# Eight attention steps left undivided, their sums turned by TensorE and multiplied into the values

## The chip, the cores and the metric

The kernel runs on one core of a Trainium2 chip. A core has five engines that each work through a queue of their own in order: TensorE (PE in the profile, its weight loads PEld), VectorE (DVE), ScalarE (ACT), GpSimd (POOL) and SyncE (SP), which here issues nearly all the DMAs. [...] The metric is the time of one execution on the device in microseconds (us), as the median of several runs.

## The reference

```python
scale = 1.0 / np.sqrt(q.shape[-1])
scores = scale * np.matmul(q, k.transpose(0, 1, 3, 2))
thresh = np.max(scores, axis=-1, keepdims=True) - tau
scores = np.where(scores >= thresh, scores, -1000000000.0)
scores = scores - np.max(scores, axis=-1, keepdims=True)
attn = np.exp(scores)
attn = attn / (np.sum(attn, axis=-1, keepdims=True) + 1e-09)
return np.matmul(attn, v).astype(np.float32)
...
x = np.ascontiguousarray(attn_out.transpose(0, 2, 1, 3)).reshape(B * S, H * D)
h = x @ w_in
g = np.where(h > 0.0, h, alpha * (np.exp(np.minimum(h, 0.0)) - 1.0))
return (g @ w_out).astype(np.float32)
```

There are 8 sequences of 8 heads, 576 tokens and a head dimension of 64. Scores that lie more than tau under the maximum of their row are dropped; the rest goes through a softmax. The result, 4608 tokens by 512, goes through a network with 2048 hidden units and an ELU. All is fp32. The division by the sum is the line that the change touches: a row of weights is divided by its own sum, and then multiplied by the values.

## The kernel before, in words

Two heads of a sequence form a pair (`pr`, 32 in all). A step `(pr, i)` is a block of 128 queries of both heads; `i` is 0 to 3 for the four whole blocks and 4 (`NC`) for the 64 queries of each head that are left, which share one block. A step does this: TensorE makes the scores (`scores`, L673), VectorE the maximum of each row (`max_of`, L730). Then a row is masked in one of two forms, chosen for each step and head by the set `MASK_ACT`:

- VectorE's form: the threshold on GpSimd (`bound_of`, L734), the exponential on ScalarE (`exp_of`, L768), and on VectorE a compare-and-multiply that also sums the row (`mask_of`, L775).
- ScalarE's form: the threshold on VectorE (`pivot_of`, L746 or L748), a steep Prelu on ScalarE that sinks what lies under the threshold (`sink_of`, L753), and on ScalarE again an exponential that also sums the row (`raise_of`, L759). Here the Prelu needs the threshold, so it waits for VectorE twice: for the maximum, and for the threshold made from it.

The two sums are added up with a tiny constant (`total_of`, L783, or `total_act`, L720) and turned over (`reciprocal_of`, L789). Each head's 128x576 weights are multiplied by 1/sum on GpSimd (L726), ScalarE (`ACT_NORM`, L714) or VectorE (`NORM_DVE`, L709). TensorE turns the weights by 128x128 transposes (`turn_parts`, L792) in three parts, and each part is copied out of PSUM (a task called `put`, L808), by ScalarE or, for the parts in the set `PUT_DVE`, by VectorE. When all the steps of half a pair have their turned weights, TensorE multiplies them by the values (`values`, L925 and L930), and ScalarE copies the result to the tile `xt` (`values_out`, L1060), from which the network's first product reads.

In the first sequence the steps are ordered by their number n: n = 0 to 7 are blocks 0 and 1 of the pairs 0 to 3, n = 8, 9, 10 are blocks 2, 3 and 4 of pair 0, and so on. The first product of the network on the first 256 tokens (`ffn1`, L1102) can start once the values of n = 0 to 7 are there. Beside the steps, the 64-bit weights of the network are loaded and made fp32 in 32 pieces (tasks `lw`, `rest`, `shift`, `add`, `sign`, `end`; L485 to L518).

What is done when is fixed before the run. `early_tasks` gives every task a due time, from a formula plus entries of the table `MOVED`, sorts by it, and issues the tasks in that order; a task first issues all those that it needs, so a task with a late due time comes in just before the first task that needs it. The order in which tasks are issued is the order in which each engine's queue holds their instructions. In the stretch that matters below, the order by due time is: the maxima of step 6 (both heads), `end` of weight piece 0, the third part of step 4 with the copy out of pair 1's values, then `mask` of (6, 0) at 53, `mask` of (6, 1) at 54, and the three `put`s of step 5 at 55. The threshold of (6, 1) has the due time 914, so it is issued when `mask` of (6, 1) asks for it.

PSUM sets two more orders. Transposed parts and values share a pool of two buffers (tag `rt`): `room_for` issues whatever empties the older buffer before it gives out a new one.

```python
def room_for(pool, release):
    while len(taken[pool]) >= 2:
        taken[pool].popleft()()
    taken[pool].append(release)
```

So the third part of a step waits for the copy of the first part, and the values for an earlier part's copy. The scores have three buffers, one for each head: the scores of a step wait until the mask (VectorE's form) or the Prelu (ScalarE's form) has read the buffer's last content. `IDLES` puts some spare transposes of a constant into TensorE's queue.

Of the kernel before, what the change touches and what calls it, by code (L numbers as in the profile page):

```python
# [10 lines left out]
FP32 = mybir.dt.float32  # L11
# [4 lines left out]
ALU = mybir.AluOpType  # L16
# [7 lines left out]
 (7, 2)}  # L24
SU_ACT = {3, 13, 15, 20, 23, 25, 26, 29, 30, 31, 32, 33, 34, 35, 37, 39, 44}
QK_PE = set()
MASK_ACT = {(0, 0), (0, 1), (1, 1), (2, 0), (7, 1), (8, 0), (9, 1), (12, 1), (13, 0), (14, 1), (15, 0), (15, 1), (17, 0),
# [11 lines left out]
SCALE_ACT = {3, 6, 7, 9}  # L39
SUM_POOL = {0, 3}  # L40
SPLIT = {(4, 10)}
PUT_DVE = {(0, 2), (6, 2), (12, 0), (12, 1), (14, 1), (14, 2), (16, 1), (17, 2), (20, 1), (21, 0), (26, 0), (29, 0), (33,
 1), (33, 2), (34, 1)}

HEADS_APART = {(0, 0), (0, 1)}
# [323 lines left out]
def kernel(  # L369
# [22 lines left out]
    KJ = DM // P  # L392
    NFT = DF // P
    NPAIR = H // 2
# [8 lines left out]
    xpool = ctx.enter_context(tc.tile_pool(name="xpool", bufs=2))  # L403
# [312 lines left out]
    def total_act(pr, i, hs):  # L716
# [2 lines left out]
        st["summed"] = True  # L719
        nc.scalar.activation(st["su"][:, cs], st["sm"][:, cs, 0], AF.Identity, bias=st["sm"][:, 0, 1:2])  # L720

    def normalize(pr, i, hs):
        st = open_steps[pr, i]
        for h in hs:
            wv = st["w"][:, h * S : (h + 1) * S]
            nc.gpsimd.tensor_scalar(wv, wv, st["rs"][:, h : h + 1], 1.0, ALU.mult, ALU.mult)  # L726
# [64 lines left out]
    def transpose(dst, src):  # L791
        nc.tensor.matmul(dst, src, idents[-1], is_transpose=True, skip_group_check=True)  # L792
# [104 lines left out]
    def fetch(pr, i):  # L897
# [11 lines left out]
        else:  # L909
# [2 lines left out]
                back.rearrange("k (a b) n -> k a b n", b=2),  # L912
            )

    def values(pr, part, pv=None):
        b, j = divmod(pr, NPAIR)
        vm, vd = (raws[pr][x] for x in ("vm", "vd"))
        wT = wTs.pop((pr, part))
        if b not in xts:
            xts[b] = xpool.tile([P, KJ, MAIN], FP32, name="xt")  # L920
        n = wT.shape[1] * T
        if pv is None:
            pv = psum["t"].tile([P, 512], FP32, name="pv", tag="rt")
        watch = on_banks if wide else lambda *a: None
        watch(nc.tensor.matmul(pv[:, :n], vd, wT[:, :, NC], start=True, stop=False, skip_group_check=True), pv[:, :n])  # L925
        for c in range(NC):
            for h in range(2):
                g0, g1 = (2 * h, 2 * h + 10) if part else (0, 2 * NT)
                o = pv[h * D : (h + 1) * D, g0 * T : g1 * T]
                watch(nc.tensor.matmul(o, vm[:, h, c], wT[:, g0:g1, h * (NC + 1) + c], start=False, stop=(c == NC - 1),  # L930
                                       skip_group_check=True), o)
        return lambda: values_out(pr, part, pv)

    wide, turned_by = [], []
# [120 lines left out]
    def values_out(pr, part, pv):  # L1055
        b, j = divmod(pr, NPAIR)
        q0, n = TAIL * part, (3 if part else 2) * NT * T
        watch = on_banks if wide else lambda *a: None
        o = pv[:, q0 : q0 + 2 * P]
        watch(nc.scalar.copy(xts[b][:, j, part * 2 * P : (part + 1) * 2 * P], o), o)  # L1060
# [114 lines left out]
    steps = [(pr, i) for pr in range(NP) for i in ((0, 1, NC, 2, 3) if pr >= JOINED else range(NB))]  # L1175
    steps[:per_seq] = [(pr, i) for x in ((0, 1), (2, 3, NC)) for pr in range(NPAIR) for i in x]
    LATE = 10

    def behind(pr, i):
        if i in (1, NB - 1):  # L1180
# [126 lines left out]

    def early_tasks():
# [161 lines left out]
        for n in range(MIDDLE):  # L1470
# [16 lines left out]
            for h in hs:  # L1487
                task(("max", n, h), at_(0.2 + 0.5 * h, 1.8 + 0.6 * h, 0.8 + 0.5 * h), f"max{h}{k}", lambda pr=pr, i=i, h=h: max_of(pr, i, h), ("sc", n))
                back = ("turned", n - (2 if last_ else WBUFS)) if n >= WBUFS else None
                t_exp, t_th, t_mask = (at_(0.3 + 0.7 * h, 2.0 + 0.6 * h, 1.0 + 0.5 * h), at_(0.4 + 0.7 * h, 2.2 + 0.6 * h, 1.1 + 0.5 * h),  # L1490
                                       at_(2.0 + 1.6 * h, 5.6 + 0.1 * h, 4.0 + 0.1 * h))
                if (n, h) in MASK_ACT:
                    task(("exp", n, h), t_exp, f"exp{h}{k}", lambda pr=pr, i=i, h=h: sink_of(pr, i, h), ("th", n, h), back, "late" if last_ else None)
                    task(("th", n, h), t_th, f"th{h}{k}", lambda pr=pr, i=i, h=h: pivot_of(pr, i, h), ("max", n, h))
                    task(("mask", n, h), t_mask, f"mask{h}{k}", lambda pr=pr, i=i, h=h: raise_of(pr, i, h), ("exp", n, h))
                else:
                    task(("exp", n, h), t_exp, f"exp{h}{k}", lambda pr=pr, i=i, h=h: exp_of(pr, i, h),
                         ("max", n, h), exps[-1] if exps else None, ("mask", *exps[-2][1:]) if len(exps) > 1 else None)
                    task(("th", n, h), t_th, f"th{h}{k}", lambda pr=pr, i=i, h=h: bound_of(pr, i, h), ("max", n, h))
                    exps.append(("exp", n, h))  # L1500
                    task(("mask", n, h), t_mask, f"mask{h}{k}", lambda pr=pr, i=i, h=h: mask_of(pr, i, h), ("exp", n, h), ("th", n, h),
                         ("mask", n, 0) if h and (n, 0) not in MASK_ACT else back, "late" if last_ else None)
                scaled = normalize_act if (n, h) in ACT_NORM else normalize_dve if (n, h) in NORM_DVE else normalize_pool
                norm = lambda pr=pr, i=i, h=h, f=scaled: f(pr, i, h)
                task(("norm", n, h), at_(5.0 + 0.8 * h, 6.2 + 0.1 * h, 5.4 + 0.1 * h), f"norm{h}{k}", norm, ("rec", n))
            task(("su", n), at_(3.8, 5.8, 4.4), f"su{k}", lambda pr=pr, i=i, hs=hs, f=total_act if n in SU_ACT else total_of: f(pr, i, hs), *[("mask", n, h) for h in hs])
            task(("rec", n), at_(3.8, 5.8, 4.4), f"rec{k}", lambda pr=pr, i=i, hs=hs: reciprocal_of(pr, i, hs), ("su", n))
# [37 lines left out]
            if i in (1, NC) and n < MIDDLE - 4:  # L1545
                got = []
                mine_ = [number[pr, x] for x in ((0, 1) if i == 1 else (2, 3, NC))]

                def run_values(pr=pr, part=part, got=got):
                    room_for("t", lambda: do(("out", pr, part)))  # L1550
                    got.append(values(pr, part))

                def run_out(pr=pr, part=part, got=got):
                    got[0]()
                    if (pr, part) == (NPAIR - 1, 0):
                        push_ffn(0)
                    elif (pr, part) == (NPAIR - 1, 1):
                        push_ffn(1)

                m = n + 2  # L1560
                t_val, t_out = (begin[m] + 4.0, begin[m] + 6.2) if m < LATE else (begin[m] + 0.4, begin[m] + 3.3)
                if n < per_seq:
                    t_val, t_out = begin[n + 1] + 4.2, begin[n + 2] + 1.5
                    if n >= LATE:
                        t_val, t_out = begin[n + 1] + 5.6, begin[n + 1] + 6.8
                elif any(m in SQUARES for m in mine_):
                    t_val, t_out = begin[n + 3] + 5.7, begin[n + 3] + 5.8
                elif SWITCH + 1 >= m >= SWITCH:
                    t_val, t_out = t_val - 8.0, t_out - 8.0
                task(("val", pr, part), t_val, f"val{k}", run_values, *[("landed", m) for m in mine_], ("v", pr))  # L1570
                task(("out", pr, part), t_out, f"out{k}", run_out, ("val", pr, part), ("out", pr, 0) if part else None)
            if n == 0:
                task("idle", t + 2.1, None, lambda: idle(16))
            if n >= SWITCH:
# [777 lines left out]
```

## Time and profile before

| what | value |
|---|---|
| median of 3 runs | 1259.22 us (1258.13 to 1260.99) |
| the profiled execution's own time | 1259.32 us |
| span from its first to its last instruction | 1257.5 us |
| PE, DVE, ACT, POOL busy, share of the span | 99%, 83%, 51%, 58% |
| first matmul of the network (L1102) | 51.48 us |

The profile is of one execution. It gives busy times of each engine, the groups of instructions with their mean duration, the instructions in order of time with the idle time ahead of them and what ended it, and the chain of waits: the work that ended last, followed back link by link. Times in its rows count from the start of the span. "f" is a PSUM bank of the network, "sc" scores, "e" exponentials, "w" weights of the attention, "wTa" and "wTb" turned weights, "pv" values, "rt" turned parts, "mx" maxima, "th" thresholds, "rs" 1/sum.

### The profile page before, as it was taken

To read this page: it belongs to the slowest core of one execution; us is meant where nothing else is said; L and a number is where in the kernel's file an instruction comes from. 1 tells how busy PE (TensorE), PEld (TensorE's weight loads), DVE (VectorE), ACT (ScalarE), POOL (GpSimd) and SP (SyncE) were. 2 spreads that over 40 slices of the span, in tenths; PEclk is the share of its full clock that TensorE was granted. 3 is DMA by queue.
4 is the path that set the end of the run, shared out by engine and by line. 5 is a ranking of instruction groups with operands and counts; after the bars stand their busy time and mean duration, and the time that the engine had idled before them with its cause. 6 is when DMAs were issued, how large, how long until landed. Compare 5 with 4: busy or idle time off the path is not lost.

```text
span 1257.5 us, 21116 instructions
## 1 busy us (share of the span) xinstructions
PE 1243.9 (99%) x6598; PEld 957.0 (76%) x6598; DVE 1040.3 (83%) x2199; ACT 635.2 (51%) x1331; POOL 727.1 (58%) x1061
## 2 busy tenths in 40 slices
PE   8999999999999999999999999999999999999998
PEld 6676576467878787888778787878788887788886
DVE  7888778789798988898889879898889876776983
ACT  7989776664352526253534435252625353465330
POOL 4778655687475847666576747584766655122000
PEclk9999999999999999999999999999999999999999
DMA  7557688998889898998989998999889885000001
GB/s 134 151 177 177 177 244 234 260 248 216 239 239 266 245 240 224 241 263 228 252 206 253 237 231 231 256 257 240 228 238 262 221 241 175 20 1 1 1 34 34
DMA packets 325551, 245.74 MB, mean 195 GB/s; under 512 B 209216, under 2 KB 289984, under 8 KB 325440
## 3 DMA queue, kind: packets, MB, share of 16 engines
q1 hardware_dynamic: 323264, 243.65, 72.2%
q8 instruction: 52, 0.85, 0.3%
q10 hardware_dynamic: 2176, 0.75, 0.2%
q14 instruction: 59, 0.48, 0.1%
HBM read 154.53 MB, written 89.78 MB: 194 GB/s over the span
## 4 chain that ended last, share of the span: by engine, by line
PE 90%; DVE 3%; DMA 2%; ACT 2%; issue 1%; SPq 1%; POOL 1%; DVEq 0%; ACTq 0%; POOLq 0%
PE f L1678 23%; PE f L1818 22%; PE sc L977 8%; PE sc L1050 7%; PE f L2278 7%; PE f L2203 5%; PE f L1102 4%; PE sc L673 3%; PE f L1154 3%; PE f L2216 2%; PE pv L930 2%; PE rt L792 1%; PE sc L1042 1%; PE sc L1037 1%; DMA there<-x 1%
## 5 line engine op out<-in xcount | busy, mean ns | idle before, releaser
L984 DVE TENSOR_REDUCE mx<-sc 128x1 f32<-128x576 f32 x207 | 148.3, 750 | 28.5 <-PE sc L977 24.6
L726 POOL TENSOR_SCALAR w<-w,rs 128x576 f32<-128x576 f32 x144 | 115.8, 813 | 70.0 <-DVE rs L789 69.8
L1004 ACT ACTIVATE w<-sc,mx 128x576 f32<-128x576 f32 x113 | 81.5, 740 | 116.0 <-DVE mx L984 98.7
L868 DVE STREAM_TRANSPOSE x<-w 128x512 f32<-128x512 f32 (+1 forms) x153 | 108.9, 744 | 15.3 <-POOL w L726 11.3
L996 POOL TENSOR_SCALAR th<-mx,ntau 128x2 f32<-128x2 f32 (+1 forms) x114 | 33.8, 297 | 133.3 <-DVE mx L984 133.3
L977 PE MATMUL sc<-kT,qT 64*128 64x448 f32 (+4 forms) x736 | 103.4, 416 | 0.2 <-ACT xs L1066 0.2
L977 PEld LDWEIGHTS sc<-kT,qT 64*128 64x128 f32 x736 | 81.0, 186 | 25.1 <-issue 16.5
L1011 DVE SCALAR_TENSOR_TENSOR w<-sc,th,w 128x576 f32<-128x576 f32 x113 | 88.2, 811 | 9.4 <-ACT w L1004 9.2
L1678 PE MATMUL f<-xt,sw 128*128 128x256 f32 x384 | 93.8, 386 | 1.8 <-DVE g L1700 1.8
L1678 PE MATMUL f<-xt,w_in 128*128 128x256 f32 x384 | 92.2, 382 | 0.0
L1818 PE MATMUL f<-w_out,s 128*128 128x256 f32 x384 | 92.0, 382 | 0.1
L1818 PE MATMUL f<-w_out,g 128*128 128x256 f32 x384 | 92.0, 382 | 0.0
L1678 PE MATMUL f<-x,w_in 128*128 128x256 f32 x384 | 90.9, 379 | 0.0
L1818 PE MATMUL f<-t,s 128*128 128x256 f32 x384 | 90.8, 379 | 0.0
L726 POOL TENSOR_SCALAR e<-e,rs 128x576 f32<-128x576 f32 x91 | 67.1, 741 | 35.6 <-DVE rs L789 34.2
L1678 PEld LDWEIGHTS f<-xt,sw 128*128 128x128 f32 x384 | 69.4, 189 | 18.6 <-issue 4.8
L1678 PEld LDWEIGHTS f<-xt,w_in 128*128 128x128 f32 x384 | 71.7, 190 | 12.7 <-ACT w L1692 2.2
L1818 PEld LDWEIGHTS f<-w_out,g 128*128 128x128 f32 x384 | 72.0, 190 | 12.4 <-issue 3.1
L1818 PEld LDWEIGHTS f<-w_out,s 128*128 128x128 f32 x384 | 71.9, 190 | 12.4 <-issue 2.5
L1678 PEld LDWEIGHTS f<-x,w_in 128*128 128x128 f32 x384 | 72.8, 190 | 10.5 <-ACT s L1692 0.6
L1818 PEld LDWEIGHTS f<-t,s 128*128 128x128 f32 x384 | 72.8, 190 | 10.3 <-POOL s L1765 0.4
L1765 POOL TENSOR_TENSOR s<-g 128x256 f32<-128x256 f32 x96 | 74.9, 785 | 7.9 <-DVE g L1728 7.5
(316 smaller groups left out, 3103.5 us busy)
## 6 DMA issues: line engine op xcount, KB each, us to landing
there<-x SPq DMA_DIRECT2D x444, 144.0 KB, 3.5
wTb<-there SPq DMA_DIRECT2D x58, 576.0 KB, 6.5
wTa<-there SPq DMA_DIRECT2D x53, 576.0 KB, 5.0
sw<-win_sums SPq DMA_DIRECT2D x46, 384.0 KB, 4.9
t<-wout_sums SPq DMA_DIRECT2D x33, 512.0 KB, 6.2
qm<-in_q_dram SPq DMA_DIRECT2D x124, 72.0 KB, 4.9
wst<-in_moe_w_in_dram SPq DMA_DIRECT2D x16, 512.0 KB, 4.4
vm<-in_v_dram SPq DMA_DIRECT2D x64, 128.0 KB, 3.9
```

Of the source, the lines that this page charges most:

```text
L726: nc.gpsimd.tensor_scalar(wv, wv, st["rs"][:, h : h + 1], 1.0, ALU.mult, ALU.mult)
L868: nc.vector.transpose(x[:, :, c0 : c0 + nc_], src.rearrange("p (c g n) -> p g c n", c=nc_, n=T))
L977: on_banks(nc.tensor.matmul(o, qT[r, i * P : (i + 1) * P], kT[r, k0 : k0 + n], start=True, stop=True, skip_group_check=True), o)
L984: on_banks(nc.vector.tensor_reduce(st["mx"][:, h : h + 1], st["sc", h], axis=AX.XY if i == NC else AX.X, op=ALU.max, negate=True), st["sc" ...
L1004: on_banks(nc.scalar.activation(st["e", h], st["sc", h], AF.Exp, bias=st["mx"][:, h : h + 1]), st["sc", h])
L1011: on_banks(nc.vector.scalar_tensor_tensor(st["e", h], st["sc", h], st["th"][:, h : h + 1], st["e", h], ALU.is_ge, ALU.mult, accum_out=st[" ...
L1050: on_banks(nc.tensor.matmul(o, vm[:, h, c], parts[part][:, g0:g1, h * (NC + 1) + c], start=False, stop=(c == NC - 1), skip_group_check=Tru ...
L1678: nc.tensor.matmul(loc["banks"][place], left[:, j], right[:, j], start=(begins and j == 0), stop=(j == 1), skip_group_check=True)
L1765: engine.tensor_tensor(o, x, y, op)
L1818: nc.tensor.matmul(place(m), lhs, rhs, start=(begins and v == 0), stop=(v == RU - 1), skip_group_check=True)
L2203: nc.tensor.matmul(o, w.rearrange("p (j f) -> p j f", j=KJ)[:, j], m, start=(j == 0 and x == 0), stop=(j == KJ - 1 and x == 1), skip_group ...
L2278: nc.tensor.matmul(banks8[2 * i + x // 2], h[:, tok], w, start=(f == 0 and x != 1), stop=(f == NFT - 1 and x != 0), skip_group_check=True)
```

## The change

For the steps n = 0 to 7 (the list `UNSCALED` of half pairs) the weights are no longer multiplied by 1/sum. In place of the task `norm` of head 0, GpSimd writes 1/sum of both heads 64 times over into a 128x128 tile (`widen`); `norm` of head 1 does nothing. Just before the values of a pair, TensorE turns the two tiles of its two steps into one PSUM buffer of the pool `rt` (task `spread`), so that partitions hold the output's rows and the free dimension the queries. ScalarE copies these 128x256 numbers to the place in `xt` where the result will lie (task `scales`), and VectorE multiplies the values in PSUM by them into that same place, instead of ScalarE's copy of the values.

Three sets change beside it: the masks (5, 1) and (6, 1) take ScalarE's form, and the copies of the third part of steps 0 and 6 move from VectorE to ScalarE. `MOVED` stays as it is, and `spread` and `scales` have a due time so late that they come in when the values, the next buffer or the output ask for them.

```diff
-MASK_ACT = {(0, 0), (0, 1), (1, 1), (2, 0), (7, 1), (8, 0), ...
+MASK_ACT = {(0, 0), (0, 1), (1, 1), (2, 0), (5, 1), (6, 1), (7, 1), (8, 0), ...
-PUT_DVE = {(0, 2), (6, 2), (12, 0), ...
+PUT_DVE = {(12, 0), ...
+    def widen(pr, i):
+        st = open_steps[pr, i]
+        st["wide"] = wstage.tile([P, 2, D], FP32, name="rsd", bufs=3)
+        nc.gpsimd.tensor_copy(st["wide"], st["rs"].unsqueeze(2).broadcast_to([P, 2, D]))
...
+    scales = {}
+
+    def spread(pr):
+        rt = psum["t"].tile([P, 512], FP32, name="rt", tag="rt")
+        for i in range(2):
+            transpose(rt[:, i * P : (i + 1) * P], open_steps[pr, i]["wide"].rearrange("p h d -> p (h d)"))
+        return rt
+
+    def keep_spread(pr, rt):
+        b, j = divmod(pr, NPAIR)
+        if b not in xts:
+            xts[b] = xpool.tile([P, KJ, MAIN], FP32, name="xt")
+        scales[pr] = xts[b][:, j, : 2 * P]
+        nc.scalar.copy(scales[pr], rt[:, : 2 * P])
...
-        watch(nc.scalar.copy(xts[b][:, j, part * 2 * P : (part + 1) * 2 * P], o), o)
+        if (pr, part) in UNSCALED:
+            nc.vector.tensor_tensor(xts[b][:, j, : 2 * P], o, scales.pop(pr), ALU.mult)
+        else:
+            watch(nc.scalar.copy(xts[b][:, j, part * 2 * P : (part + 1) * 2 * P], o), o)
...
+    UNSCALED, LAST = [(pr, 0) for pr in range(NPAIR)], 9000.0
...
+                if (pr, int(i >= 2)) in UNSCALED:
+                    norm = (lambda: None) if h else lambda pr=pr, i=i: widen(pr, i)
...
+                    def run_spread(pr=pr, got_spread=got_spread):
+                        room_for("t", lambda: do(("scales", pr)))
+                        got_spread.append(spread(pr))
+
+                    task(("spread", pr), LAST, None, run_spread, *[("rec", m) for m in mine_])
+                    task(("scales", pr), LAST, None, lambda pr=pr, got_spread=got_spread: keep_spread(pr, got_spread[0]),
+                         ("spread", pr), ("out", pr - 1, 0) if pr else None)
-                task(("val", pr, part), t_val, f"val{k}", run_values, *[("landed", m) for m in mine_], ("v", pr))
-                task(("out", pr, part), t_out, f"out{k}", run_out, ("val", pr, part), ("out", pr, 0) if part else None)
+                task(("val", pr, part), t_val, f"val{k}", run_values, *[("landed", m) for m in mine_], ("v", pr),
+                     ("spread", pr) if (pr, part) in UNSCALED else None)
+                task(("out", pr, part), t_out, f"out{k}", run_out, ("val", pr, part),
+                     ("out", pr, 0) if part else ("scales", pr) if (pr, 0) in UNSCALED else None)
```

More of the change, by code (lines that the diff above doesn't have):

```diff
@@ L26 @@
 QK_PE = set()
-MASK_ACT = {(0, 0), (0, 1), (1, 1), (2, 0), (7, 1), (8, 0), (9, 1), (12, 1), (13, 0), (14, 1), (15, 0), (15, 1), (17, 0),
+MASK_ACT = {(0, 0), (0, 1), (1, 1), (2, 0), (5, 1), (6, 1), (7, 1), (8, 0), (9, 1), (12, 1), (13, 0), (14, 1), (15, 0), (15, 1), (17, 0),
  (20, 0), (20, 1), (21, 0), (21, 1), (22, 0), (23, 0), (24, 0), (25, 0), (25, 1), (26, 0), (26, 1), (27, 0), (27, 1), (28,
@@ L41 @@
 SPLIT = {(4, 10)}
-PUT_DVE = {(0, 2), (6, 2), (12, 0), (12, 1), (14, 1), (14, 2), (16, 1), (17, 2), (20, 1), (21, 0), (26, 0), (29, 0), (33,
+PUT_DVE = {(12, 0), (12, 1), (14, 1), (14, 2), (16, 1), (17, 2), (20, 1), (21, 0), (26, 0), (29, 0), (33,
  1), (33, 2), (34, 1)}
@@ L1569, in early_tasks @@
                     t_val, t_out = t_val - 8.0, t_out - 8.0
-                task(("val", pr, part), t_val, f"val{k}", run_values, *[("landed", m) for m in mine_], ("v", pr))
-                task(("out", pr, part), t_out, f"out{k}", run_out, ("val", pr, part), ("out", pr, 0) if part else None)
+                if (pr, part) in UNSCALED:
+                    got_spread = []
+                    def run_spread(pr=pr, got_spread=got_spread):
[8 more added lines that the diff above has]
+                     ("out", pr, 0) if part else ("scales", pr) if (pr, 0) in UNSCALED else None)
             if n == 0:
```

## The prediction

> **What bounds the kernel now.** I read the page first, then the busy time by stretches, then the chain of waits, and last the instructions in order of time on three engines. The stretches show, in columns, length, PE, PEld, DVE, ACT and POOL busy, granted clock, DMA share and GB/s.
>
> ```profile
> span 1257.5 us, 21116 instructions
> 8.67:58.47 49.80, 45.52 (x293) 31.39 (x294) 41.05 (x95) 46.07 (x89) 34.21 (x50) 1.00 0.65 154
> 36.73:42.42 5.69, 5.69 (x41) 3.67 (x41) 4.60 (x12) 4.96 (x10) 3.76 (x6) 1.00 0.46 148
> 62.82:212.30 149.48, 149.48 (x755) 97.56 (x756) 120.59 (x256) 121.62 (x254) 102.47 (x123) 1.00 0.75 198
> ```
>
> From 62.82 to 212.30 TensorE has no gap at all: a delay or gain that stands at 62.82 goes through to the end, as all later work is issued behind it. The change lies ahead of that, in the first 52 us, where no engine is full. ScalarE comes nearest, with 46.07 of 49.80 us. So there the links decide:
>
> ```profile
> 12.63 1.33 POOL w L726 x2
> 14.07 0.75 POOL x L584
> ...
> 28.30 0.53 DVE w L709
> ...
> 33.71 0.75 DVE mx L730
> 34.54 0.62 ACT e L768
> 35.21 0.74 ACT e L768
> ...
> 36.80 1.17 PE sc L673 x8
> ...
> 40.48 1.32 PE sc L673 x8
> ...
> 42.42 0.59 ACT wTb L808
> ...
> 51.47 1.77 POOL w L726 x2
> ...
> 62.82 1.59 PE sc L673 x8
> ```
>
> The reader is to see two things. Only two links are normalizations of the first eight steps (12.63 and 28.30; the one at 51.47 is of step 9 and stays). And from 33.71 to 42.42 the chain is tight: maximum of (6, 0), both exponentials of step 6, a copy, the scores of step 7, then TensorE without a gap (5.69 of 5.69) through the values of pair 2 and the scores of step 8.
>
> **The change, part by part.** Prices first.
>
> ```profile
> L726 POOL TENSOR_SCALAR w<-w,rs 128x576 f32<-128x576 f32 x144 | 115.8, 813 | 70.0 <-DVE rs L789 69.8
> L629 POOL COPY kT<-kT 64x64 f32<-64x64 f32 x30 | 7.0, 235 | 8.9 <-DVE su L783 4.6 <-DVE kT L590 3.4
> L714 ACT ACTIVATE w<-w,rs 128x576 f32<-128x576 f32 x38 | 29.1, 773 | 6.7 <-DVE rs L789 6.7
> L1060 ACT COPY xt<-pv 128x256 f32<-128x256 f32 x16 | 5.8, 365 | 2.2 <-PE pv L930 2.1
> L808 ACT COPY wTb<-rt 128x128 f32<-128x128 f32 x9 | 2.4, 263 | 1.3 <-PE rt L792 1.3
> L1836 DVE TENSOR_TENSOR ot<-f,u 128x256 f32<-128x256 f32 x24 | 10.0, 417 | 2.8 <-PE f L1818 2.8
> 1.48 4.66 PE L792 MATMUL rt<-ident 128*128 128x128 f32 x22 [1.48 <-POOL ident masks.py:199]
> 10.72 1.97 PE L792 MATMUL rt<-ident 128*128 128x128 f32 x16
> ```
>
> *Sixteen multiplications go* (11 on GpSimd, 4 on ScalarE, 1 on VectorE), and 8 widening copies come on GpSimd. No row shows a broadcast 128x128 copy; it lies between 0.235 (64x64) and 0.813 us (128x576), and I take 0.3, as its 128 elements lie nearer to 64. At every such place GpSimd has less to do than before, and nobody waits for the copy but `spread`: cost nothing. No DMA moves, and neither SP's queue nor GpSimd's DMAs are passed by anything.
>
> *The two links on the chain.* At 12.63 the scaling of pair 1's queries (14.07) no longer stands behind two multiplications. It then waits for VectorE's transposition, which ends at 12.47 + 0.78 = 13.25 by the first row below: 0.8 us sooner. Of that, 0.2 goes to the third copy of step 0, now in ScalarE's queue ahead of step 2's Prelu (0.263 less the overlap), and 0.1 to `spread` of pair 0, which must wait for the copy ahead of the last one; 0.5 stays. At 28.30 the multiplication of (4, 0) goes: 0.4, together 0.9 us sooner at ScalarE's exponentials of step 5. But (5, 1) in ScalarE's form puts a second exponential into ScalarE's queue ahead of the scaling of pair 3's queries (31.50), for which step 6's scores wait. It takes 0.77 (from 40.55 to 41.32 below). Remainder: 0.13 sooner, between 0 and 0.9 if the scaling turns out not to be what step 6 waits for. I take 0.15.
>
> ```profile
> 12.47 0.78 DVE L577 STREAM_TRANSPOSE x<-qm 128x576 f32<-128x576 f32 x1
> 31.50 0.78 ACT L582 ACTIVATE qT<-qT,keep 128x576 f32<-128x576 f32 x1
> 33.69 1.42 DVE L730 TENSOR_REDUCE mx<-sc 128x1 f32<-128x576 f32 x2 [0.36 <-PE sc L673]
> 35.03 0.69 DVE L518 SCALAR_TENSOR_TENSOR w_in<-wtop,wst 128x512 f32<-128x512 f32 x1
> 35.80 0.82 DVE L775 SCALAR_TENSOR_TENSOR w<-sc,th,e 128x576 f32<-128x576 f32 x1
> 39.46 0.21 DVE L746 TENSOR_SCALAR th<-mx,ntau 128x1 f32<-128x1 f32 x1
> 35.84 1.26 ACT L808 COPY wTa<-rt 128x512 f32<-128x512 f32 x3
> 40.55 0.78 ACT L759 ACTIVATE w<-w,ntau 128x576 f32<-128x576 f32 x1
> 41.32 0.35 ACT L1060 COPY xt<-pv 128x256 f32<-128x256 f32 x1
> 34.74 1.04 PE L792 MATMUL rt<-ident,w 128*128 128x128 f32 x8
> 36.48 0.33 PE L792 MATMUL rt<-ident,w 128*128 128x128 f32 x1 [0.70 <-ACT wTa L808]
> ```
>
> *The mask (6, 1) in ScalarE's form: the added wait.* Before, ScalarE goes from the exponential of (6, 0) at 34.54 straight to that of (6, 1) at 35.21. After, it is a Prelu that needs a threshold made on VectorE; and by the due times (`mask` of (6, 0) at 53, of (6, 1) at 54, the threshold only when (6, 1) asks) that threshold stands in VectorE's queue behind the mask of (6, 0). VectorE's order becomes: both maxima (33.69), weight piece 0 (35.03 to 35.80), the multiplication of pair 1's values (new; 0.417 less the 0.07 by which neighbours overlap, 0.35), the mask of (6, 0) (from 36.15, not 35.80; 0.82 less the same overlap, to 36.90), the threshold (0.21). The Prelu starts at 37.1, not 35.21: 1.9 us in which ScalarE stands still with the copies of step 5 behind it. Then comes the second exponential, 0.77. The copies at 35.84 come 1.9 + 0.77 = 2.65 us later. TensorE's third part of step 5 (36.48) already waits for the first of them now, and the scores of step 7 stand behind it. Bounds: 0.77, if ScalarE never waits, to 3.1, if the multiplication takes twice its row.
>
> *`spread` and the values.* Two transposes at 0.123 (1.97 / 16) are 0.25, with their PSUM turn 0.3. For pair 2 they lie on TensorE's gapless stretch: +0.3 (0 to 0.5). For pairs 0, 1 and 3 they fill a wait for a copy that is there now, such as the 0.35 at 47.29 below; if that cover went, 0.25 each. A values' matmul of pair 1 now also waits for step 4's first copy, which ends ahead of it anyhow. The four copies of 1/sum on ScalarE (0.365 each) take the place of its four copies of the values.
>
> ```profile
> 47.29 0.70 PE L925 MATMUL pv<-wTb,vd 128*128 128x256 f32 x2 [0.35 <-ACT wTb L808]
> 49.80 0.66 PE L792 MATMUL rt<-ident,w 128*128 128x128 f32 x4
> 48.95 0.42 DVE L494 TENSOR_SCALAR wtop<-wst 128x512 uint32<-128x512 uint32 x1
> 49.46 0.82 DVE L775 SCALAR_TENSOR_TENSOR w<-sc,th,e 128x576 f32<-128x576 f32 x1
> 50.93 0.16 DVE L783 TENSOR_REDUCE su<-sm 128x2 f32<-128x4 f32 x1 [0.64 <-ACT w L759]
> 62.41 0.41 PE L792 MATMUL rt<-ident,w 128*64 128x128 f32 x2 [0.52 <-ACT wTb L808]
> ```
>
> *From 42 to 62.* ScalarE gets step 6's third copy and pair 3's 1/sum ahead of step 9's mask: 0.2 + 0.3. VectorE's multiplication for pair 3 waits until the values end (49.80 now, about 0.15 later then) with step 9's mask (49.46 now) behind it: 49.95 + 0.35, then the weight instruction that stands at 48.95 now (0.42) with its neighbours' small waits, mask at 50.85, done at 51.65, where the sum of step 9 starts at 50.93 now: +0.75 (0 to 1.0). GpSimd's multiplications of step 9 (51.47) wait for that sum, and the chain goes from them to 62.82; TensorE has only 0.52 us of idle time there (62.41) to give.
>
> *The sum.* -0.15 + 2.65 + 0.3 + 0.75 = +3.55 us. The execution profiled took 1259.32 us, 1.8 around its span and 0.1 over the median of 1259.22: 1262.9 us, 0.3% slower. A change under about 0.2%, 2.5 us, can't be told from none.
>
> [...] TensorE would stand idle from 34.74 + 1.04 = 35.8 to 36.48 + 2.65 = 39.1, some 3.3 us. The rows at 1.48 and 10.72 show the same transposes at 212 ns at the start and 123 ns later, and short gaps, as the 0.70 at 36.48, are not followed by slow ones. [...]
>
> **The rivals.**
>
> *No standstill at (6, 1).* If ScalarE finds the threshold ready, as for (7, 1) at 39.46, only the second exponential's 0.77 comes in: -0.15 + 0.77 + 0.3 + 0.75 = +1.7, 1261.0 us. The due times speak against it.
>
> *Faster: ScalarE's work sets the early stage.* It idles 49.80 - 46.07 = 3.7 us between 8.67 and 58.47, mostly for copies and maxima that stand behind the multiplications. It loses 4 multiplications (L714, 0.773 less some 0.1 of overlap, 2.7) and gains two copies and two exponentials (0.4 + 1.54): -0.75. With half of its idle time gone too it is -2.6: 1256.7 us. It decides if the new standstill is caught up before 42.42, which needs a gap on TensorE from 36.73 to 42.42; the row shows none.
>
> *The clock falls in the gap.* The 22 transposes at the start took 22 x (212 - 123) ns = 1.96 us more than warm ones. That much on top gives 1264.8 us. For it: the length of the gap. Against: no clock below 1.00 in any stretch.
>
> **How the numbers follow.** Standstill as summed 0.54, with a range of its own from 1261.3 to 1264.0; no standstill 0.20; faster 0.15; clock 0.11. The time is the first one's, 1262.9. From 1257.5 to 1264.9 leaves out most of the faster case (0.12) and half of the clock case (0.06). Bounds of 0.2% lie at 1256.7 and 1261.7: faster 0.12; within, the second rival, the rest of the faster case and about a sixth of the first: 0.31; slower 0.57.
>
> **What would show it.** In the profile after: between ScalarE's exponential of (6, 0) and the Prelu of (6, 1) an idle time near 2 us that a threshold of L746 ends; the scores of step 7 near 39.3, not 36.80; TensorE's first matmul of the network 2.5 to 3 us later than in the table before; the group L1060 with four fewer, four multiplications of 0.42 us on VectorE. The prediction is wrong if that Prelu waits under 0.5 us, or if the gap at 39 is there and the scores of step 12 come less than 2 us after 62.82.

## The result, and the profile after

The changed kernel takes 1264.05 us (1263.52 to 1265.26) where the kernel before takes 1258.51 us (1258.12 to 1260.99) on the same chip: 1.0041 times as long, 95% interval 1.0030 to 1.0052. The profiled execution took 1263.52 us, against 1259.32 us before. The forecast was 1262.9 us, in a range from 1257.5 to 1264.9.

The span and the busy times by stretches of the changed kernel (columns as before: length, PE, PEld, DVE, ACT, POOL, granted clock, DMA share, GB/s):

```profile
span 1261.7 us, 21121 instructions
```

```profile
8.67:58.47 49.80, 42.08 (x266) 28.19 (x267) 36.22 (x86) 40.56 (x82) 21.84 (x40) 0.97 0.58 133
...
40.00:45.00 5.00, 5.00 (x30) 2.77 (x28) 2.43 (x5) 2.56 (x5) 2.04 (x3) 0.72 0.02 6
...
62.82:212.30 149.48, 149.48 (x766) 99.23 (x763) 121.38 (x255) 123.22 (x257) 102.08 (x122) 1.00 0.73 196
```

In the early stage every engine is less busy than before, TensorE by 3.4 us (42.08 for 45.52), ScalarE by 5.5; 266 of TensorE's matmuls fall into it instead of 293, so a part of this is work that now comes later. The loss is idle time, and one new thing: a granted clock of 0.72 in one stretch, where no stretch of the kernel before was below 1.00. From 62.82 on TensorE is without a gap in both kernels.

The chain of waits of the changed kernel, where the kernel before had both exponentials of step 6 at 34.54 and 35.21, a copy, and the scores of step 7 at 36.80:

```profile
36.24 0.73 DVE w L780 x2
...
37.14 0.75 ACT w L758
...
37.91 0.87 ACT w L764 x2
38.78 0.48 ACT wTa L813
...
39.30 0.46 PE rt L797
39.77 2.22 PE sc L673 x8
```

ScalarE's second exponential of step 6 has become a Prelu (L758) and an exponential (L764), and ahead of it stands VectorE's mask of (6, 0). The scores of step 7 start at 39.77 instead of 36.80, and they take 2.22 us where they took 1.17. The instructions behind it, in order of time, first ScalarE, then VectorE, then TensorE:

```profile
37.14 0.74 ACT L758 ACTIVATE w<-sc,th 128x576 f32<-128x576 f32 x1 [1.72 <-DVE th L751]
```

```profile
35.83 0.42 DVE L1081 TENSOR_TENSOR xt<-pv,xt 128x256 f32<-128x256 f32 x1
36.16 0.81 DVE L780 SCALAR_TENSOR_TENSOR w<-sc,th,e 128x576 f32<-128x576 f32 x1
...
36.89 0.21 DVE L751 TENSOR_SCALAR th<-mx,ntau 128x1 f32<-128x1 f32 x1
...
54.60 0.43 DVE L1081 TENSOR_TENSOR xt<-pv,xt 128x256 f32<-128x256 f32 x1 [0.99 <-PE pv L950]
...
56.20 0.16 DVE L788 TENSOR_REDUCE su<-sm 128x2 f32<-128x4 f32 x1
```

```profile
32.62 1.24 PE L673 MATMUL sc<-kT,qT 64*128 64x288 f32 x8 [0.26 <-ACT qT L582]
...
36.30 0.66 PE L797 MATMUL rt<-ident,w 128*128 128x128 f32 x4 [0.19 <-DVE xt L1081]
39.30 0.46 PE L797 MATMUL rt<-ident,w 128*128 128x128 f32 x1 [2.35 <-ACT wTa L813]
39.70 2.29 PE L673 MATMUL sc<-kT,qT 64*128 64x288 f32 x8
41.92 0.69 PE L797 MATMUL rt<-ident,rsd 128*128 128x128 f32 x2
...
43.11 1.95 PE L950 MATMUL pv<-wTa,vm 128*64 128x256 f32 x16
...
56.24 1.21 PE L673 MATMUL sc<-x,qd 128*128 128x288 f32 x4 [1.17 <-DVE w L780]
57.28 1.89 PE L1125 MATMUL f<-xt,w_in 128*128 128x256 f32 x8
...
67.84 1.65 PE L673 MATMUL sc<-x 64*128 64x288 f32 x8
```

The reader is to see three places. At 37.14 the Prelu has waited 1.72 us for the threshold, which came behind multiplication and mask on VectorE; TensorE then has waited 2.35 us at 39.30 (0.70 before). At 39.70 and 41.92 TensorE is slow: 2.29 us for scores that take 1.24, and 0.69 for two transposes that take 0.44 elsewhere. At 56.24 TensorE waits 1.17 us for the mask of step 9, a wait that was not there before; VectorE had been waiting 0.99 us at 54.60 for the values of pair 3.

The same work of TensorE in the kernel before:

```profile
32.42 1.24 PE L673 MATMUL sc<-kT,qT 64*128 64x288 f32 x8
...
36.73 1.24 PE L673 MATMUL sc<-kT,qT 64*128 64x288 f32 x8
...
38.53 1.95 PE L930 MATMUL pv<-wTa,vm 128*64 128x256 f32 x16
...
62.75 1.66 PE L673 MATMUL sc<-x 64*128 64x288 f32 x8
```

How late it is in the changed kernel: scores of step 6 0.20 us (32.62 for 32.42), of step 7 2.97 (39.70 for 36.73), values of pair 2 4.58 (43.11 for 38.53), first matmul of the network 5.80 (57.28 for 51.48), scores of step 12 5.09 (67.84 for 62.75). The two profiled executions differ by 4.20 us in the end; but the one before lay 1.2 us above the median of 31 later runs of that kernel (1258.15), so that this alone does not show that anything is given back behind 62.82 (the section on the prediction takes this up).

### The profile page after: what moved, and what is told of

The parts are those of the page before. It is cut to its first block, busy times and chain, and to the rows that moved or that the text cites. A ratio compares the mean times of both kernels' runs of the same rounds, so it can differ in the third digit from the quotient of the medians.

```text
span 1261.7 us, 21121 instructions
## 1 busy us (share of the span) xinstructions
PE 1245.9 (99%) x6606; PEld 959.0 (76%) x6606; DVE 1040.3 (82%) x2198; ACT 634.8 (50%) x1333; POOL 719.9 (57%) x1056
## 4 chain that ended last, share of the span: by engine, by line
PE 90%; DVE 3%; DMA 3%; ACT 2%; SPq 2%; issue 1%; POOL 0%; DVEq 0%; ACTq 0%; POOLq 0%
PE f L1856 23%; PE f L1716 21%; PE sc L997 7%; PE sc L1070 7%; PE f L2316 7%; PE f L2241 5%; PE f L1125 5%; PE sc L673 3%; PE f L1177 3%; PE f L2254 2%; PE pv L950 2%; PE rt L797 1%; DMA there<-x 1%; PE sc L1062 1%; DVE x L873 1%; PE sc L1057 1%
## 5 line engine op out<-in xcount | busy, mean ns | idle before, releaser
L731 POOL TENSOR_SCALAR w<-w,rs 128x576 f32<-128x576 f32 x133 | 107.4, 816 | 62.7 <-DVE rs L794 62.7
```

## The experiments

All twelve are edits of the kernel after or of the kernel before. "Net" below is the shift of TensorE's work against the kernel before, less the shift that is there already at the transposes at 10.72, which differs by up to 0.6 us from one execution to the next; these transposes start ahead of the first edited instruction.

| run | median us | against before (95%) | scores of step 7, net | of step 12, net | clock 40 to 45 |
|---|---|---|---|---|---|
| after | 1264.05 | 1.0041 (1.0030 to 1.0052) | +2.98 | +5.10 | 0.72 |
| e1 mask (6, 1) back | 1261.00 | 1.0021 (1.0011 to 1.0030) | +0.32 | +1.18 | 1.00 |
| e2 threshold early | 1260.75 | 1.0017 (1.0007 to 1.0026) | +1.28 | +2.14 | 1.00 |
| e3 gap filled | 1262.18 | 1.0028 (1.0018 to 1.0038) | +2.84 | +3.69 | 1.00 |
| e4 undivided alone | 1261.04 | 1.0020 (1.0011 to 1.0030) | -0.17 | +0.68 | 1.00 |
| e5 sets alone | 1264.48 | 1.0055 (1.0042 to 1.0068) | +3.57 | +5.14 | 0.66 |
| e13 mask (6, 1) alone | 1262.64 | 1.0028 (1.0016 to 1.0039) | +2.50 | +4.14 | 0.66 |
| e12 sets, threshold early | 1262.58 | 1.0029 (1.0019 to 1.0038) | +2.34 | +2.44 | 1.00 |
| e6 after, pair 3 later | 1263.91 | 1.0048 (1.0036 to 1.0061) | +2.83 | +4.86 | 0.66 |
| e7 e4, pair 3 later | 1259.93 | 1.0014 (1.0005 to 1.0023) | +0.72 | +1.37 | 1.00 |
| e8 e2, pair 3 later | 1260.29 | 1.0015 (1.0006 to 1.0024) | +2.01 | +2.65 | 1.00 |
| e9 pair 0 alone | 1258.54 | 1.0002 (0.9993 to 1.0011) | -0.37 | -0.34 | 1.00 |
| e10 pairs 0 and 1 | 1259.39 | 1.0005 (0.9996 to 1.0014) | +0.55 | +0.57 | 1.00 |

The traces of e7, e8 and e12 hold a slow spell of the clock at 11 us as well (last section), so their net shifts are to be taken with care.

### The standstill: e1, e2, e3

The theory: the added mask (6, 1) makes ScalarE wait for a threshold, TensorE waits for ScalarE, and its clock falls on top. Rivals: the whole loss comes from the undivided steps; or the clock fell for another reason than the gap. e1 takes the mask back, e2 only alters where the threshold stands in VectorE's queue, e3 leaves the wait and gives TensorE spare transposes in it.

```diff
 e1, against after
-MASK_ACT = {..., (5, 1), (6, 1), (7, 1), ...
+MASK_ACT = {..., (5, 1), (7, 1), ...
 e2, against after
-"th_6_1": 882.9
+"th_6_1": 17.4
 e3, against after
-IDLES = {(2, 2, 2), (5, 0, 9), (6, 1, 3), ...
+IDLES = {(2, 2, 2), (5, 0, 9), (5, 1, 20), (6, 1, 3), ...
```

> The changed kernel with the mask (6, 1) alone back in VectorE's form. Theory of the standstill (ScalarE waits 1.72 us for the threshold of (6, 1), TensorE's gap of 2.35 us follows, and its clock falls behind the gap): ScalarE goes from the exponential of (6, 0) straight to that of (6, 1), the scores of step 7 start within 0.5 us of where they start in the kernel before (now +2.97), the clock stays at 1.00 from 40 to 45 (now 0.72), the values of pair 2 lie at about +0.5 (now +4.49), and the time is 4 us under the changed kernel's, 1259.5 to 1260.5. Rival (leaving the weights undivided is what costs, by the turned sums and the multiplication in VectorE's queue): within 1 us of the changed kernel's 1264.

> The changed kernel with one VectorE instruction moved: the threshold of (6, 1) stands right behind the maximum of (6, 1), ahead of weight piece 0, the multiplication and the mask of (6, 0). All other queues are as in the changed kernel. Theory of the standstill: the Prelu of (6, 1) waits under 0.3 us (now 1.72), only the second exponential is left (0.77), the scores of step 7 start at +1.0 to +1.5, the clock stays at 1.00, and the time is 2.5 to 3.5 us under the changed kernel's, 1260.5 to 1261.5. If it is ScalarE's extra work and not the order on VectorE, the time stays within 1 us of 1264.

> The changed kernel with 20 spare transposes in TensorE's gap, ahead of the second part of step 5; the standstill of ScalarE stays. If the clock falls because TensorE stands idle: the scores of step 7 still start near +3, but take 1.2 us and not 2.3, the granted clock from 40 to 45 is 1.00 and not 0.72, the values of pair 2 lie at +3.2 and not +4.49, and the time is 1.2 to 1.5 us under the changed kernel's, about 1262.6. If the long scores come from something else (a PSUM buffer, weights that land late), they stay at 2.3 us and the time at 1264.

ScalarE and the stretch of 40 to 45 us with the threshold early (e2):

```profile
35.47 0.74 ACT L758 ACTIVATE w<-sc,th 128x576 f32<-128x576 f32 x1 [0.17 <-DVE th L751]
```

```profile
40.00:45.00 5.00, 5.00 (x38) 3.21 (x37) 3.85 (x10) 4.44 (x8) 2.82 (x4) 1.00 0.01 2
```

The Prelu waits 0.17 us instead of 1.72, and 3.3 us go (1264.05 to 1260.75), more than the wait itself: with it goes the slow spell. In e1, without the Prelu, 3.05 us go. With the gap filled (e3) TensorE has these two rows in place of the wait of 2.35:

```profile
36.22 2.40 PE L797 MATMUL rt<-ident 128*128 128x128 f32 x20 [0.19 <-DVE xt L1081]
...
39.22 0.33 PE L797 MATMUL rt<-ident,w 128*128 128x128 f32 x1 [0.17 <-ACT wTa L813]
39.48 1.24 PE L673 MATMUL sc<-kT,qT 64*128 64x288 f32 x8
```

The scores of step 7 are as late as in the changed kernel (39.48), but take 1.24 us; the net shift of step 12 falls from 5.10 to 3.69, the time by 1.9 us, somewhat more than the 1.2 to 1.5 expected (the ratios, 1.0041 and 1.0028, have intervals that overlap; the rows of the two profiled executions show it plainly). So the gap brings the slow clock here, and the clock is worth some 1.4 us in the trace.

e2 came as expected (1260.5 to 1261.5 us). e1 did not: 1259.5 to 1260.5 us were expected, and it stays 2.9 us above the kernel before, as e2 stays 2.6 above it. So the standstill at (6, 1) is not the whole loss.

### What is left: e4 and e5

e4 has the undivided steps with the three sets as before, e5 the three sets on the kernel before.

```diff
 e4, against after
-MASK_ACT = {..., (5, 1), (6, 1), (7, 1), ...
+MASK_ACT = {..., (7, 1), ...
-PUT_DVE = {(12, 0), ...
+PUT_DVE = {(0, 2), (6, 2), (12, 0), ...
 e5, against before
-MASK_ACT = {..., (7, 1), ...
+MASK_ACT = {..., (5, 1), (6, 1), (7, 1), ...
-PUT_DVE = {(0, 2), (6, 2), (12, 0), ...
+PUT_DVE = {(12, 0), ...
```

> Only the undivided steps: both masks in VectorE's form and both copies on VectorE as in the kernel before. Theory of the standstill: no clock under 1.00, the scores of step 7 0.3 to 0.8 us ahead of the kernel before, then +0.3 for the turned sums of pair 2 and about +1.2 where step 9's mask stands behind the multiplication: 1258.5 to 1260. Rival (the undivided steps cost): 1262 to 1264.

> The kernel before with the two masks (5, 1) and (6, 1) in ScalarE's form and the two copies moved to ScalarE; all weights are divided as before. Theory of the standstill: the threshold of (6, 1) stands behind the mask of (6, 0) here too, without a multiplication ahead of it, so the Prelu of (6, 1) waits 1.3 to 1.6 us, TensorE waits 2.5 to 3 us ahead of the scores of step 7, and the time is 1260.4 to 1262.0 us, 2.3 to 3.8 over before. Rival (the sets cost only in company of the undivided steps, whose multiplication holds up the mask of (6, 0)): 1258.2 to 1259.2 us. If the granted clock falls in 40 to 45 us as in the changed kernel, another 0.8 to 1.5 us is on top.

e4 takes 1261.04 us, 2.9 over before, between what was expected (1258.5 to 1260) and what the rival gave (1262 to 1264). e5 takes 1264.48, 6.3 over before: about 1 us above even the 1261.2 to 1263.5 that the expected range gives with the fall of the clock, which came here too. The parts do not add up: 2.9 + 6.3 is 9.2, the whole change is 5.5. TensorE in e5:

```profile
34.05 1.24 PE L673 MATMUL sc<-kT,qT 64*128 64x288 f32 x8 [0.99 <-ACT qT L582]
...
40.47 0.33 PE L792 MATMUL rt<-ident,w 128*128 128x128 f32 x1 [3.01 <-ACT wTa L808]
```

Without the undivided steps the second exponential of (5, 1) holds up the scaling of pair 3's queries, and the scores of step 6 wait 0.99 us for it at 34.05; in the changed kernel they wait 0.26 (32.62), as the undivided steps had brought that scaling forward by 1.0 us (31.80 for 33.24, of which 0.44 is the later start of e5's trace). The wait ahead of step 7 is 3.01 us, longer than the 2.35, although no multiplication stands ahead of the mask here.

### One mask alone, and the sets with the threshold early: e13 and e12

```diff
 e13, against before
-MASK_ACT = {..., (2, 0), (7, 1), ...
+MASK_ACT = {..., (2, 0), (6, 1), (7, 1), ...
 e12, against before: the edits of e5, and
-"th_6_1": 882.9
+"th_6_1": 17.4
```

> The kernel before with the one mask (6, 1) in ScalarE's form and nothing else. With all of the sets but no undivided step the time was 1264.48 us, TensorE waited 3.01 us ahead of the scores of step 7, and its clock fell to 0.66 in 40 to 45 us. Theory of the standstill: this mask alone makes most of that. The threshold stands behind the mask of (6, 0) in VectorE's queue, the Prelu waits 1.3 to 1.5 us, the second exponential adds 0.77, TensorE waits 2.6 to 3.0 us where it waited 0.70, the clock falls again, and the time is 1261.6 to 1263.2 us. Rival (the other mask and the two copies matter as much): 1259.2 to 1260.5 us.

> The sets alone (1264.48 us) with the threshold of (6, 1) made right after the maxima, ahead of the mask of (6, 0). Theory of the standstill: the wait of 1.44 us ahead of the Prelu goes, TensorE's wait falls from 3.01 to 1.5 to 1.9 us, the clock stays at 1.00 in 40 to 45 us, and the time falls by 2.3 to 3.3 us, to 1261.2 to 1262.2; what stays over before is the second exponentials of (5, 1) and (6, 1), 0.77 us each, and the copies. Rival (the exponentials alone keep the gap long enough for the clock to fall): 1263.0 to 1264.0 us.

TensorE in e13, and its granted clock in stretches of 1 us:

```profile
39.18 0.33 PE L792 MATMUL rt<-ident,w 128*128 128x128 f32 x1 [3.24 <-ACT wTa L808]
39.44 1.24 PE L673 MATMUL sc<-kT,qT 64*128 64x288 f32 x8
...
41.72 3.09 PE L930 MATMUL pv<-wTa,vm 128*64 128x256 f32 x16
```

```profile
40.00:41.00 1.00, 1.00 (x7) 0.59 (x4) 0.29 (x1) 1.00 (x2) 0.00 (x0) 0.84 0.10 33
41.00:42.00 1.00, 1.00 (x4) 0.35 (x5) 1.00 (x2) 0.53 (x2) 0.42 (x2) 0.50 0.00 0
...
43.00:44.00 1.00, 1.00 (x8) 0.56 (x6) 0.17 (x2) 0.97 (x3) 1.00 (x2) 0.50 0.03 8
44.00:45.00 1.00, 1.00 (x10) 0.54 (x8) 0.16 (x1) 0.24 (x3) 1.00 (x2) 0.96 0.00 0
```

One entry in a set costs 3.8 us (1262.64 for 1258.85 of the kernel before, run beside it): 2.50 by the wait and another 1.63 by the clock, which falls only after the scores of step 7 have run at full rate; net 4.14 at the scores of step 12. That was expected, TensorE's wait a little shorter than it is (2.6 to 3.0, measured 3.24). What e5 has over this, the mask (5, 1) and the two copies, is 1.0 us net at the scores of step 12 (5.14 for 4.14) and 2.5 us by the times, so the rival holds a part of the truth.

With the threshold early the sets alone fall to 1262.58 us. The same wait on TensorE, and the clock behind it:

```profile
38.71 0.33 PE L792 MATMUL rt<-ident,w 128*128 128x128 f32 x1 [1.78 <-ACT wTa L808]
```

```profile
40.00:45.00 5.00, 5.00 (x37) 3.33 (x36) 3.63 (x9) 4.10 (x8) 3.58 (x5) 1.00 0.03 10
```

Wait and clock are as expected; the time is 0.4 us above the range that was given. Against the kernel before, run beside it (1258.85), it is +3.7 us, 2.6 us less than e5's +6.3.

### Pair 3's multiplication: e6, e7, e8

The wait of 1.17 us at 56.24 looked like the next cost: the multiplication of pair 3 waits for its values, with the mask of step 9 behind it. Each of the three kernels has it behind mask, sum and reciprocal of step 9.

```diff
 e6 against after, e7 against e4, e8 against e2
-"out_3_0": 31.5
+"out_3_0": 38
```

> The changed kernel with one due time altered, so that the multiplication of pair 3's values stands in VectorE's queue behind the mask, the sum and the reciprocal of step 9. In the changed kernel this multiplication waits 0.99 us for TensorE's values (at 54.60), the mask of step 9 stands behind it (55.27), and TensorE waits 1.17 us for that mask ahead of the scores of step 10 (56.24). Queue theory: that wait goes or falls below 0.3 us, the scores of step 10 and the first matmul of the network come 0.8 to 1.3 us sooner, and the time is 1262.7 to 1263.3 us against 1264.05. Rival (the remaining loss lies in the turned sums, two transposes and a copy for each pair): the time stays within 0.3 us of 1264.05. Second rival (first network matmul waits for the later multiplication): the wait moves from 56.24 to 57.28, and the time stays too.

> The first eight steps undivided without the two masks and the two copies in ScalarE's form (the run that took 1261.04 us), with pair 3's multiplication behind the mask, sum and reciprocal of step 9. Queue theory: most of the 2.9 us that were left over come from that one place in VectorE's queue, of which 1.17 us is TensorE's wait at 52.39: 1259.6 to 1260.2 us. Rival (each pair pays for its turned sums and its multiplication alike, some 0.7 us a pair): 1260.8 to 1261.3 us.

> The changed kernel with both places in VectorE's queue altered: the threshold of (6, 1) ahead of the mask of (6, 0), and pair 3's multiplication behind the mask, sum and reciprocal of step 9. The first alone took 1260.75 us (1.0017 of before). If pair 3's place is worth the 1.1 us by which 1259.93 lies under 1261.04 with the undivided steps alone, the time is 1.0006 to 1.0012 of before. If it is worth nothing, as the traces say (the sum of step 9 then waits for ScalarE's exponential, and TensorE waits again further on, at about 64 us), it is 1.0014 to 1.0022 of before; the scores of step 10 come 0.8 us sooner than with the threshold alone, those of step 12 do not.

VectorE and TensorE in e6:

```profile
56.01 0.16 DVE L788 TENSOR_REDUCE su<-sm 128x2 f32<-128x4 f32 x1 [0.72 <-ACT w L764]
```

```profile
55.44 1.21 PE L673 MATMUL sc<-x,qd 128*128 128x288 f32 x4
...
67.53 0.41 PE L797 MATMUL rt<-ident,w 128*64 128x128 f32 x2 [0.63 <-ACT wTb L813]
```

TensorE's wait is gone and the scores of step 10 come 0.8 us sooner (55.44 for 56.24), 1.06 us net, as expected. But the time is 1263.91 us, and the theory is refuted: the sum of step 9 now waits 0.72 us for ScalarE's exponential and comes only 0.45 us sooner net (56.01 for 56.20), GpSimd's two multiplications behind it end 0.15 us sooner net (58.81 for 58.70), and TensorE waits 0.63 us again at 67.53, a place at which the changed kernel has no wait. Of the 1.06 us at step 10, 0.24 are left at step 12. A wait on TensorE that lies ahead of another chain's end was worth next to nothing. e8 against e2 says the same (1.0015 and 1.0017). e7 lies 1.1 us under e4, but they were not run beside each other and their intervals overlap; from the scores of step 7 to those of step 12 the net shift grows by 0.65 us in e7 and by 0.85 in e4, so the rows show 0.2 us of it. Its expectation was hit in number only.

### Which pairs cost: e9 and e10

```diff
 against e4
-    UNSCALED, LAST = [(pr, 0) for pr in range(NPAIR)], 9000.0
+    UNSCALED, LAST = [(0, 0)], 9000.0                (e9)
+    UNSCALED, LAST = [(0, 0), (1, 0)], 9000.0        (e10)
```

> Only the two steps of pair 0 are undivided; sets as in the kernel before. With all four pairs undivided, TensorE is 0.9 us sooner at 13.4 than before, against the start of its own run, since the scaling of pair 1's queries no longer stands behind two multiplications on GpSimd. Queue theory: that gain belongs to pair 0 and the losses to pairs 1 to 3, so the shift is -0.9 at 13.4 and stays below zero up to 29: 1257.3 to 1258.3 us. Rival (each pair pays some 0.7 us): 1258.6 to 1259.2 us. Third possibility: the gain at 13.4 is taken up by the link through VectorE's normalization at 28.30, and the time is that of the kernel before, 1258.1.

> Pairs 0 and 1 undivided, pairs 2 and 3 divided, sets as before. Pair 0 alone took 1258.54 us, all four pairs 1261.04. If pairs 2 and 3 carry the loss (their turned sums stand in TensorE's gapless stretch after 36.7 us, and the multiplication of pair 3 holds up step 9's mask): 1258.3 to 1259.0 us. If pair 1 carries it (its multiplication stands ahead of the mask of (6, 0), at 35.90): 1259.4 to 1260.2 us.

With pair 0 alone TensorE is 0.9 us sooner net at 13.43, 0.7 at the values of pair 1, and 0.34 at the scores of step 12; the time, 1258.54, is that of the kernel before within its interval. It is the best of these kernels and beats nothing; the number lies between what the first theory and the rival gave. The third possibility has the time, but not the reason: 0.7 us of the gain is still there behind the link at 28.30. With pair 1 added the time is 1259.39 us, between the two cases; against the kernel before that ran beside it (1258.85) it is 0.5 over, where the edge of the first case was 0.8 and that of the second 1.2 over 1258.17. The values of pair 1 are 1.0 us later than with pair 0 alone, net +0.32 for -0.69. TensorE in e10:

```profile
28.88 0.38 PE L797 MATMUL rt<-ident,rsd 128*128 128x128 f32 x2
29.72 0.70 PE L945 MATMUL pv<-wTb,vf 128*128 128x256 f32 x2 [0.46 <-ACT wTa L813]
```

The values wait 0.46 us for ScalarE's copy of step 4's first part, for which they do not wait with pair 0 alone (29.21, no wait). The turned sums take one more buffer of the pool of two, so by the order of `room_for` the values must wait for one more copy; no run tests this alone. From the start of step 4's first part to the values it is 1.30 us in e10 (28.42 to 29.72) and 0.46 in e9. So the gain belongs to pair 0 and is small; the later pairs eat it up. That pairs 2 and 3 carry most of the remaining 2.9 us of e4 rests on medians (1261.04 against 1259.39); in the traces they bring only 0.1 us net at step 12 (0.68 against 0.57). In e4's trace some 0.5 us of the rest has come by 133.51 (131.76 before, 1.2 net for 0.7 at step 12). Where the others arise stays open.

## Why the prediction was right and wrong

*Sixteen multiplications go.* Right. GpSimd's widening copy takes 0.289 us for the 0.3 that was taken, and the groups are as foretold:

```profile
L725 POOL COPY rsd<-rs 128x128 f32<-128x128 f32 x8 | 2.3, 289 | 13.1 <-DVE rs L794 11.9 <-PE rt L797 1.2
L731 POOL TENSOR_SCALAR w<-w,rs 128x576 f32<-128x576 f32 x133 | 107.4, 816 | 62.7 <-DVE rs L794 62.7
...
L1083 ACT COPY xt<-pv 128x256 f32<-128x256 f32 x12 | 4.4, 363 | 2.1 <-PE pv L950 2.1
L1081 DVE TENSOR_TENSOR xt<-pv,xt 128x256 f32<-128x256 f32 x4 | 1.7, 422 | 1.1 <-PE pv L950 1.0
```

*The two links on the chain.* -0.15 at the scores of step 6 was foretold, +0.20 came. The first link gave 0.9 us (0.8 foretold), of which the turned sums of pair 0 took 0.28: they found no wait to lie in. The second link gave its 0.4, so that TensorE was done with the first part of step 4 1.0 us sooner (28.43 for 29.42). But the values of pair 1 started only 0.2 us sooner (29.19): between lie the turned sums of pair 1 and a wait of 0.32 us for ScalarE's copy of that first part. The forecast had this copy end ahead of the values anyhow; in the kernel before it starts at 29.62, behind their start. ScalarE's exponentials of step 5 then came 0.6 us sooner (29.62 for 30.24) instead of 0.9, and the scores of step 6 waited 0.26 us for its scaling.

*The mask (6, 1): the added wait.* Right, place and size. The Prelu started at 37.14 (37.1 foretold) after 1.72 us (1.9). From the scores of step 6 to those of step 7 the shift grew by 2.77 us for the 2.65 of this term. e1, e2 and e13 show that this wait is the cause.

*TensorE's idle time and the clock.* This is where the forecast failed: the likeliest case had no fall of the clock, and the clock fell (0.72 from 40 to 45 us). The rival that held it had the chance of 0.11, with 1264.8 us as its time; 1264.05 was measured. That chance was an estimate: what gap brings a fall was shown by no trace of the kernel before. The price, 1.96 us, was taken from the 22 transposes at 1.48, at 212 ns each on average; the granted clock reads 1.00 there (from 2 to 5 us), so no row shows that the clock made them slow. In the rows the fall costs 1.05 us at the scores of step 7 and 0.25 at the turned sums, 1.3 together, 1.4 by e3 and 1.6 in e13. The argument against it was that no stretch had a clock below 1.00; but no stretch had such a gap either, and the forecast had worked out a gap of 3.3 us. The gap was 2.35 us, since TensorE's last transposes ahead of it were themselves held up until 36.95, and the clock fell behind it.

*`spread` and the values.* 0.28 us for pair 2, 0.3 foretold, of which the 0.05 for the turn in PSUM was an estimate that no row shows by itself. That pair 0 fills a wait was wrong, see above.

*From 42 to 62.* 0.75 us foretold. From the values of pair 2 to the scores of step 12 the shift grew from 4.58 to 5.09, by 0.5. The size is near, the reason given holds in part only. The forecast had VectorE's multiplication hold up the sum of step 9; it did, and TensorE's scores of step 10 as well, which was not foretold (1.17 us at 56.24). But e6 shows that without it the sum is only 0.45 us sooner net and the scores of step 12 only 0.24, since ScalarE's exponential ends last then.

*The sum.* In the profiled shift at the scores of step 12 it was +3.55 for +5.09; some 1.4 of the 1.5 that lacked is the clock. That the time fell into the range is luck in part. The range of the likeliest case ended at 1264.0 us, and 1264.05 lies in the part that was kept for the rival on the clock. The base helped too: 1259.32 us lay above the later median of 1258.15, so the increase was missed by 2 us (5.5 for 3.55) and the time by 1.15.

*The rivals.* No standstill: out, the Prelu waited 1.72 us. Faster: out; ScalarE was idle for 9.2 us of the early stage (49.80 less 40.56) instead of 3.7.

*That a shift at 62.82 stays.* In the changed kernel it does up to 212.30, as forecast. TensorE further on, first in the kernel before, then in the changed one:

```profile
211.01 1.24 PE L673 MATMUL sc<-kT,qT 64*128 64x288 f32 x8
...
271.32 1.13 PE L1678 MATMUL f<-xt,sw 128*128 128x256 f32 x4 [1.37 <-DVE g L1700]
```

```profile
216.07 1.24 PE L673 MATMUL sc<-kT,qT 64*128 64x288 f32 x8
...
275.43 1.13 PE L1716 MATMUL f<-xt,sw 128*128 128x256 f32 x4 [0.43 <-DVE g L1738]
```

The 5.09 us of step 12 are 5.06 at 216.07 and 4.11 at 275.43. The 0.95 us between lie in the last wait shown, 1.37 us before and 0.43 after: in the trace of the kernel before, VectorE waits 2.62 us for a DMA (at 269.86) ahead of it, in that of the changed kernel 1.68 (at 273.97). This wait does not follow the shift: in e9, whose TensorE is 0.34 us ahead of the kernel before net, it is 0.64 us (at 268.02). So it reads as a difference between executions, and not as loss that the kernel makes up. What later stretches add is not taken apart: the differences of the medians lie from 0.5 us under to 2.2 us over the net shift at step 12, and single executions of one kernel differ by that much (1258.12 to 1260.99).

## What to carry to other kernels

An instruction in a form that needs another engine's small result can pay for that engine's queue too (the Prelu of (6, 1) waited 1.72 us for a threshold that takes 0.21, and 0.17 us in e2): look up what stands ahead of the result there before counting the instruction's own time, and give the small result its place first. Where a new wait leaves TensorE idle for as long as here (2.34 to 3.24 us in four kernels), add the slow spell behind it to the sum, 1.4 to 1.6 us in these traces; the spare transposes of e3 in the gap took it away. And before repairing a wait, see which other chain ends at the next meeting point: the repair at 56.24 moved TensorE by 1.06 us net there and by 0.24 at step 12, and the time by nothing that can be told from noise.

## What the runs showed of the hardware

The clock's slow spell was of one length and rate in the four kernels that had it behind this gap. The granted clock in stretches of 1 us was 0.68, 0.50, 0.50, 0.62 in the changed kernel from 39 us on, 0.84, 0.50, 0.50, 0.50, 0.96 in e13 from 40 on, 0.56, 0.50, 0.50, 0.73 in e5 from 41 on, and 0.89, 0.50, 0.50, 0.50, 0.90 in e6 from 40 on. Taken as 0.50 throughout the spell and 1.00 outside it, an estimate from these stretches, the spell lasts from 39.36 to 42.76 us in the changed kernel and from 40.68 to 44.08 in e13: 3.40 us both times. In e5 and e6 it is 3.42. How long TensorE must be idle for it is not shown: its longest waits ahead of the spell were 2.35 us in the changed kernel, 2.34 in e6, 3.01 in e5 and 3.24 in e13, while 1.78 us in e12 brought no spell there, each in one execution. When the spell begins differs too: in the changed kernel with the first work behind the gap (39.30), in e13 1.5 us after TensorE had begun again, at 39.18.

The gap alone does not decide. In three executions, of e7, e8 and e12, the granted clock was 0.50 from 12 to 14 us as well, with no wait of over 1.12 us between TensorE's first matmul and that spell; the 16 transposes there took 3.1 us in e7 instead of 1.97. The stretches of e7:

```profile
10.00:12.00 2.00, 2.00 (x13) 1.60 (x12) 1.15 (x4) 2.00 (x6) 0.27 (x1) 0.81 0.84 160
12.00:14.00 2.00, 2.00 (x11) 2.00 (x11) 1.96 (x5) 1.93 (x4) 1.04 (x2) 0.50 1.06 294
```

That took about 1 us from the gain at 13.43 in the trace of e7, and is one reason why differences of under 1 us between single executions of these kernels mean little.
